# Interleaving score products with maxima products, and a row-paired output projection, in a two-path attention kernel

## The chip, the cores and the metric

The kernel runs on one core of one Trainium2 chip. The metric is the device time of one execution in microseconds (us), the median of several runs. TensorE (PE in the profile, its weight loads PEld) multiplies, VectorE (DVE) takes maxima and does arithmetic, ScalarE (ACT) does exponentials and copies, GpSimd (POOL) masks and adds, SyncE (SP) issues DMAs. Each engine works through its own instructions in their order and waits on semaphores.

## What is computed

Two attention blocks share one input x (2048 x 512, 32 heads of 16 dimensions). Path A is causal attention within four chunks of 512 tokens, plus a memory carried from chunk to chunk. Path B is full attention over all 2048 tokens. Each has its own weights and its own output projection, and a gate mixes them:

```python
logits = einsum("bhqd,bhkd->bhqk", qs, ks) * scale + mask     # A, per chunk of 512
o = g * a_mem + (1.0 - g) * softmax(logits) @ vs              # A, then  a = o @ wo
scores = einsum("bhqd,bhkd->bhqk", q, k) * (Dh ** -0.5)       # B, all 2048 tokens
b = (softmax(scores) @ v).transpose(...).reshape(B, S, D) @ wo
out = g * a + (1 - g) * b
```

## The kernel before, in words

**Units.** The work is cut into 32 units of path A and 32 of path B; a unit is four heads and 512 queries. After a first part (projections of q, k and v, about 330 us) the main loop runs k = 0 to 31; turn k does unit k of A and unit 32 + k of B.

**Groups.** A turn has 37 groups, n = 0 to 36, recorded by `t_group`. Groups 0 to 31 are of B: two groups for each of 16 tiles of 128 keys, two heads in each. Groups 32 to 36 are of A. A group of B is one *T product* for each of its two heads (L528): 64 rows of contraction (16 dimensions as a rounded part and a rest, and rows that subtract the maximum), 128 keys by 512 queries, into one PSUM bank each. Head j = 0 uses rows 0 to 63 of the array (here the *low half*), head j = 1 rows 64 to 127 (the *high half*), so that the two run side by side. ScalarE then takes the exponential of each bank (L534) into SBUF, and the bank is free again. T products use three banks in turn (tb0, tb1, mb), the one used longest ago first.

**Products with V.** `pvs` records them behind each group (L550): for the key tile before, four heads side by side in four strips of 32 columns of the array, summed over all key tiles in the bank pvb. That is another tiling of the array than that of T.

**Maxima.** The maximum that T subtracts is found one turn ahead. A *maxima task* for a unit of B (`s_b`, L474) is a pair of products, queries by 512 keys, high half first, into one of two PSUM tiles of two banks (sbk0 and sbk1, taken in turn); VectorE reduces both banks in one instruction (L476), and the tile is free again. `s_a` (L452, with mask products L456, reduced at L460 and L462) does it for A. A table `plan` gives the tasks to groups: B's 32 tasks one each to groups 20 to 31 of one turn and groups 0 to 19 of the next, A's six to groups 32 to 36. `m_chain` (L485 to L495, VectorE) joins them behind group 21, and `m_rows` transposes them on TensorE behind group 24 (L501). A group is recorded in this order: its T products, its maxima tasks, what `extras` adds, its products with V.

**Output projection.** `out_mm` (L616) does one of 24 parts, one per turn from k = 9, in group 1 (for k = 31 two): 12 products over all 128 rows of contraction into a bank of T. Odd turns do A's weights and copy the sum to SBUF (L620, ScalarE); even turns do B's, add that copy (L623, VectorE) and store the rows.

**Ends of units.** `fin_copy` (L557, VectorE) saves a unit of A in group 0 of the next turn; `fin_rec` (L574 to L578, VectorE) follows behind groups 11 and 13.

Of the kernel before, what the change touches and what calls it, by code (L numbers as in the profile page):

```python
# [7 lines left out]
FT = mybir.dt.float32  # L8
# [4 lines left out]
OP = mybir.AluOpType  # L13
# [21 lines left out]
def gated_mix_kernel(ctx, tc, xt, wq, wk, wv, wo, beta, wqkv, wob, gate_w, out):  # L35
# [477 lines left out]

    GA = (((0, (0, 1)),), ((0, (2, 3)),), ((1, (0, 1)), (3, (0, 1))), ((1, (2, 3)), (3, (2, 3))), ((2, (0, 1)), (2, (2, 3))))

    def t_group(u, n, banks):


        kd, qd, c = UN[u]
        bs = [bank(banks) for _ in range(2)]  # L520
        c0 = 0
        for it, hs in (((n // 2, (n % 2 * 2, n % 2 * 2 + 1)),) if kd == "B" else GA[n]):
            q0 = 128 * it if kd == "A" else 0
            w = C - q0
            pn = it if kd == "B" else it % 2
            for j, h in enumerate(hs):
                r = slice(64 * j, 64 * j + 64)
                nc.tensor.matmul(bs[j][:, c0:c0 + w], k_of(u, h // 2)[r, 128 * it:128 * it + 128],  # L528
                                 q_of(u)[r, h // 2, q0:], start=True, stop=True)
                PT[u, it, h] = PTILE[pn % 2][:, 2 + j if (kd, it) == ("A", 2) else h][:, c0:c0 + w]  # L530
            c0 += w
        for j in range(2):
            pt = PTILE[pn % 2][:, 2 + j if (kd, n) == ("A", 4) else hs[j]]
            nc.scalar.activation(pt, bs[j], AF.Exp, scale=SCALE)  # L534
            if kd == "A":
                m = pt[:, :128] if n < 2 else pt.rearrange("p (a t) -> p a t", a=4)[:, ::3 if n < 4 else 2]
                nc.gpsimd.affine_select(out=m, in_=m, pattern=[[1, 128]] if n < 2 else [[0, 2], [1, 128]],  # L537
                                        compare_op=OP.is_ge, fill=0.0, base=0, channel_multiplier=-1)
# [73 lines left out]
    def out_mm(c, t, a):  # L612

        b = misc()
        for n, (oi, wi, g) in enumerate([(oi, wi, g) for oi, wi in TERMS for g in range(4)]):
            nc.tensor.matmul(b, (AT["oh"], AT["ol"])[oi][:, g, a], (AT["wh"], AT["wl"])[wi][:, g, a],  # L616
                             start=n == 0, stop=n == 11)
        if a == 0:
            AT["yo"] = AT["L"].tile([128, DM], FT, name="yo")
            nc.scalar.activation(AT["yo"], b, AF.Copy)  # L620
        else:
            tt = 4 * c + t
            nc.vector.tensor_tensor(AT["yo"], b, AT["yo"], op=OP.add)  # L623
            nc.sync.dma_start(outr[tt * 128:(tt + 1) * 128, :], AT["yo"])

    def tail_ops(t):
        s = KB[2 * (t // 2)][:, t % 2]
# [247 lines left out]
    def extras(k):  # L875

        pre, post = {}, {}
        if not k:
            for n in range(4):
                pre[2 * n] = [fill[n - 4]]  # L880
        post[2 * S_LAST + 4] = [todo(m_rows, k + 1)]
        for n, at in [(k - 9, 1)] + [(23, 2 * OMI)] * (k == 31):
            if n >= 0:
                pre[at] = [todo(out_mm, n // 8, n // 2 % 4, n % 2)]
        return pre, post

    def beside(k, it):
# [35 lines left out]
    for k in range(31):  # L923
        if k:
            spread([todo(s_b, 33 + k, *t) for t in (sorted(ST_B, key=lambda t: t[2]) if k == 1 else ST_B)],
                   [(k - 1, n) for n in range(2 * S_FIRST, 2 * NT)] + [(k, n) for n in range(2 * S_LAST)])
        else:
            spread(st33[EARLY:], sorted([(0, n) for n in range(2 * S_LAST)] + [(0, 2 * n) for n in range(4)]))
        for n, t in enumerate(ST_A):
            plan.setdefault((k, 2 * NT + n - (n > 2)), []).append(todo(s_a, k + 1, *t))  # L930

    for k in range(32):
        ua, ub = k, 32 + k
        banks = T3 + [b[:, 0] for b in SBK] * (k == 31)
        for n in range(NG):
            it = n // 2 if n < NG - 1 else NT + 2
            t_group(*(ub, n) if n < 2 * NT else (ua, n - 2 * NT), banks)
            for f in plan.get((k, n), []) + ex[k][0].get(n, []):
                f()
            pvs(k, n)  # L940
            for f in ex[k][1].get(n, []):
                f()
            if n % 2 == 0 and n < NG - 1:
                continue
            beside(k, it)
            if it == S_LAST:
                m_chain(k + 1)
            if it == 4 and not k:
                late()
            if it == 4 and not k:  # L950
                load_q(ub + 2)
                for c in range(NC4):
                    load_kb(2, c)
            if it == NT and k < 29:
                load_q(ub + 3)
                load_kb(k + 3)
            if it == 6 and k < 31:
                load_q(ua + 1)
                load_ka(ua + 1)
                if (ua + 1) % 2 == 0:  # L960
                    load_va(ua + 1)
            if it == 9:
                if k % 2 == 0 and k < 30:
                    load_vb(k // 2 + 1)
                if 1 <= k <= 4:
                    load_wo(k - 1)
# [55 lines left out]
```

## Time and profile before

| | us |
|---|---|
| median of 3 runs | 1959.55 (1957.34 to 1963.12) |
| the profiled execution | 1956.4, of which the span of its instructions is 1954.7 |
| busy in it: PE, DVE, ACT, POOL | 1930.3, 1629.9, 1433.4, 275.8 |
| granted TensorE clock | 0.999 |

In the views, a row of the timeline has the start, the time from the first start to the last end, the engine, the line, what is written from what, and the count of instructions that it joins; in brackets stands how long the engine was idle before it and for what. A TensorE product starts in the record about when its weight load starts, and its recorded length holds the time through the array, so the distance from start to start is what it costs. In the page's groups the two numbers behind the bar are the busy time and the mean length in ns of one instruction. A group of B shows as T x2 (or two rows of one), the pair of the maxima task L474 x2, and L550 x8 (four products in two passes each).

### The profile page before, as it was taken

The page shows a single profiled execution, that of the slowest core. Times are in us where ns is not written, and L with a number is a line of the kernel's source. Part 1 is how long each engine was busy: PE and PEld are TensorE (multiplying, and loading weights), DVE is VectorE, ACT ScalarE, POOL GpSimd, SP SyncE. Part 2 cuts the span into 40 slices and gives each one's busy share as a digit, 9 for nine tenths or more (in the row PEclk, how much of TensorE's full clock was granted, in tenths as well). Part 3 has the DMA queues.
Part 4 walks back from the last instruction along what each step waited for, and adds up shares of the span by engine and source line. Part 5 has one row for each costly group of instructions (what it writes and reads, how often), then busy time and mean ns, then how long its engine had stood idle before and what let it go on. Part 6 is the DMA issues. An engine that isn't in the chain of part 4 may idle for free.

```text
span 1954.7 us, 43539 instructions
## 1 busy us (share of the span) xinstructions
PE 1930.3 (99%) x17485; PEld 939.3 (48%) x17485; DVE 1629.9 (83%) x1798; ACT 1433.4 (73%) x2699; POOL 275.8 (14%) x497
## 2 busy tenths in 40 slices
PE   7999999999999999999999999999999999999999
PEld 5887777444344444444444444444444444444445
DVE  7135766899999999999999999999999999999942
ACT  4233333688888888888888888888888888888884
POOL 5201000012120101111111111111111111111022
PEclk9999999999999999999999999999999999999999
DMA  7666655644444444343435453444354444434111
GB/s 218 170 205 188 198 192 178 156 98 115 98 115 93 106 91 109 81 111 80 114 87 115 87 115 87 113 87 115 87 115 87 109 86 96 101 88 106 48 50 58
DMA packets 163790, 222.49 MB, mean 114 GB/s; under 512 B 39916, under 2 KB 90556, under 8 KB 157828
## 3 DMA queue, kind: packets, MB, share of 16 engines
q1 hardware_dynamic: 159284, 211.41, 43.7%
q0 software_dynamic: 3248, 8.03, 2.1%
q8 instruction: 138, 2.26, 0.5%
q14 instruction: 64, 0.52, 0.1%
q10 hardware_dynamic: 1056, 0.26, 0.1%
HBM read 147.95 MB, written 68.16 MB: 111 GB/s over the span
## 4 chain that ended last, share of the span: by engine, by line
PE 95%; DVE 3%; ACT 1%; SPq 1%; DMA 1%; issue 0%; DVEq 0%; ACTq 0%
PE pvb L550 33%; PE tb L528 17%; PE sbk L474 12%; PE mb L528 9%; PE tb L304 4%; PE sbk L452 3%; PE tb L616 2%; PE mb L304 2%; PE sbk L287 1%; DVE mxb L476 1%; PE tb L287 1%; PE pvb L304 1%; PE mb L616 1%; PE sbk L456 1%; PE mb L287 1%; PE pvb L287 1%
## 5 line engine op out<-in xcount | busy, mean ns | idle before, releaser
L476 DVE TENSOR_REDUCE mxb<-sbk 128x2 f32<-128x1024 f32 x1024 | 1222.3, 1222 | 67.3 <-PE sbk L474 63.1
L534 ACT ACTIVATE raw<-tb 128x512 f32<-128x512 f32 x1555 | 887.5, 598 | 152.9 <-PE tb L528 89.6
L550 PE MATMUL pvb<-raw,vb 128*17 128x256 f32 (+1 forms) x8072 | 639.3, 388 | 0.0
L534 ACT ACTIVATE raw<-mb 128x512 f32<-128x512 f32 x782 | 467.6, 598 | 79.5 <-PE tb L528 44.8
L528 PE MATMUL tb<-qb,xh 64*128 64x512 f32 x872 | 331.6, 495 | 1.7 <-ACT raw L534 1.7
L550 PEld LDWEIGHTS pvb<-raw,vb 128*17 128x17 f32 x8072 | 134.4, 95 | 340.1 <-issue 336.6
L474 PE MATMUL sbk<-xh,qb 64*128 64x512 f32 x1344 | 281.5, 395 | 2.7 <-DVE mxb L476 1.8
L528 PE MATMUL mb<-qb,xh 64*128 64x512 f32 x445 | 220.6, 496 | 0.0
L537 POOL TENSOR_SCALAR_AFFINE_SELECT raw<-raw 128x256 f32<-128x256 f32 (+1 forms) x320 | 115.5, 361 | 709.6 <-ACT raw L534 701.7
L528 PEld LDWEIGHTS tb<-qb,xh 64*128 64x128 f32 x872 | 124.7, 183 | 179.6 <-issue 89.9
L528 PE MATMUL tb<-qb,kb 64*128 64x512 f32 x470 | 179.5, 496 | 1.3 <-DVE st L314 0.8
L460 DVE TENSOR_REDUCE mx<-sbk 128x2 f32<-128x768 f32 (+1 forms) x128 | 136.7, 1090 | 22.9 <-PE sbk L456 18.3
L474 PE MATMUL sbk<-kb,qb 64*128 64x512 f32 x704 | 146.4, 398 | 0.0
L474 PEld LDWEIGHTS sbk<-xh,qb 64*128 64x128 f32 x1344 | 138.3, 186 | 7.4 <-DVE mxb L476 5.0
L528 PEld LDWEIGHTS mb<-qb,xh 64*128 64x128 f32 x445 | 81.3, 183 | 95.2 <-issue 50.4
L590 POOL TENSOR_TENSOR o<-o,d 128x512 f32<-128x512 f32 x31 | 39.7, 1281 | 545.6 <-DMA d<-rd 461.9
L528 PEld LDWEIGHTS tb<-qb,kb 64*128 64x128 f32 x470 | 68.2, 183 | 100.1 <-issue 52.6
L528 PE MATMUL mb<-qb,kb 64*128 64x512 f32 x234 | 116.1, 496 | 0.0
L550 PE MATMUL pvb<-raw,va 128*17 128x256 f32 (+2 forms) x1280 | 94.7, 384 | 0.8 <-ACT pvs L559 0.8
L452 PE MATMUL sbk<-ka,qa 64*128 64x256 f32 (+3 forms) x512 | 88.2, 358 | 1.1
L528 PE MATMUL tb<-qa,ka 64*128 64x512 f32 (+3 forms) x339 | 79.5, 372 | 0.0
L311 ACT ACTIVATE st<-tb 128x512 fp32r<-128x512 f32 x33 | 19.8, 599 | 80.2 <-DVE phi L310 40.5
(284 smaller groups left out, 1837.6 us busy)
## 6 DMA issues: line engine op xcount, KB each, us to landing
xh<-dB SPq DMA_DIRECT2D x38, 512.0 KB
vb<-vdB SPq DMA_DIRECT2D x16, 1088.0 KB
dB<-st SPq DMA_DIRECT2D x64, 256.0 KB
dA<-st SPq DMA_DIRECT2D x64, 256.0 KB
pd<-pvs SPq DMA_DIRECT2D x64, 256.0 KB
kb<-dB SPq DMA_DIRECT2D x22, 512.0 KB
xh<-dB SPq DMA_DIRECT2D x38, 256.0 KB
qb<-dB SPq DMA_DIRECT2D x64, 128.0 KB
```

The lines of the kernel that those rows point to most:

```text
L287: nc.tensor.matmul(b, lhs, WV[wi][:, k, :], start=n == 0, stop=n == 11)
L304: nc.tensor.matmul(b, WS[ws][w][wi][:, k, :], (XH, XL)[xi][c][:, k, :], start=n == 0, stop=n == 11)
L452: nc.tensor.matmul(b[:, j, c0:c0 + n], q_of(u)[r, p, i * 128:(i + 1) * 128], k_of(u, p)[r, :n], start=True, stop=False)
L460: nc.vector.tensor_reduce(m[:, :, p, i], b[:, :, :n], axis=AX.X, op=OP.max)
L474: nc.tensor.matmul(b[:, j], q_of(u)[r, p, i * 128:(i + 1) * 128], k_of(u, p)[r, kc * C:(kc + 1) * C], start=True, stop=True)
L476: nc.vector.tensor_reduce(MXB[u][:, :, p, i, kc], b, axis=AX.X, op=OP.max)
L528: nc.tensor.matmul(bs[j][:, c0:c0 + w], k_of(u, h // 2)[r, 128 * it:128 * it + 128], q_of(u)[r, h // 2, q0:], start=True, stop=True)
L534: nc.scalar.activation(pt, bs[j], AF.Exp, scale=SCALE)
L537: nc.gpsimd.affine_select(out=m, in_=m, pattern=[[1, 128]] if n < 2 else [[0, 2], [1, 128]], compare_op=OP.is_ge, fill=0.0, base=0, channe ...
L550: nc.tensor.matmul(PVB[32 * h:32 * h + E + 1, q0 + lo:q0 + hi], vt[:, it, 4 * q + h, :], pt[:, lo:hi], start=it == 0 and lo == 0, stop=it ...
L590: nc.gpsimd.tensor_tensor(o, o, d, op=OP.mult)
L616: nc.tensor.matmul(b, (AT["oh"], AT["ol"])[oi][:, g, a], (AT["wh"], AT["wl"])[wi][:, g, a], start=n == 0, stop=n == 11)
```

## The change

Two parts. First, `t_group` takes the group's maxima tasks as `between` and records them after its first T product, ahead of its second. The task's pair is high half, low half, so a group of B now reads: T low, task high, task low, T high. Groups without a task, those of A, and group 1 from k = 9 are as before. Second, for k = 9 to 30 the projection is done by `out_rows` in place of `out_mm`: 24 products of 64 rows, low and high half by turns, into the two banks of an sbk tile, in the order of the maxima tasks' tiles. The two halves of the sum are then joined outside TensorE: ScalarE copies one bank, VectorE copies or adds the other, and in even turns GpSimd adds twice ahead of the store. The maxima task of group 2 of these turns is moved to the last group (36) of the turn before, and in group 1 the projection is recorded ahead of the maxima task, no longer behind it.

```diff
-    def t_group(u, n, banks):
+    def t_group(u, n, banks, between=()):
             for j, h in enumerate(hs):
+                if j:
+                    for f in between:
+                        f()
                 r = slice(64 * j, 64 * j + 64)
                 nc.tensor.matmul(bs[j][:, c0:c0 + w], k_of(u, h // 2)[r, 128 * it:128 * it + 128],
                                  q_of(u)[r, h // 2, q0:], start=True, stop=True)
+    def out_rows(c, t, a):
+        b = rot("s", SBK)
+        for n, (oi, wi, g) in enumerate([(oi, wi, g) for oi, wi in TERMS for g in range(4)]):
+            for j in range(2):
+                r = slice(64 * j, 64 * j + 64)
+                nc.tensor.matmul(b[:, j], (AT["oh"], AT["ol"])[oi][r, g, a], (AT["wh"], AT["wl"])[wi][r, g, a],
+                                 start=n == 0, stop=n == 11)
+        if a == 0:
+            AT["y"] = [AT["L"].tile([128, DM], FT, name=n) for n in ("yo", "yp")]
+            nc.scalar.activation(AT["y"][0], b[:, 0], AF.Copy)
+            nc.vector.tensor_copy(AT["y"][1], b[:, 1])
+        else:
+            tt = 4 * c + t
+            y0, y1 = AT["y"]
+            y2 = AT["L"].tile([128, DM], FT, name="yq")
+            nc.scalar.activation(y2, b[:, 0], AF.Copy)
+            nc.vector.tensor_tensor(y1, b[:, 1], y1, op=OP.add)
+            nc.gpsimd.tensor_tensor(y0, y0, y2, op=OP.add)
+            nc.gpsimd.tensor_tensor(y0, y0, y1, op=OP.add)
+            nc.sync.dma_start(outr[tt * 128:(tt + 1) * 128, :], y0)
-                pre[at] = [todo(out_mm, n // 8, n // 2 % 4, n % 2)]
+                pre[at] = [todo(out_rows if k < 31 else out_mm, n // 8, n // 2 % 4, n % 2)]
+    for k in range(9, 31):
+        plan[k - 1, NG - 1] += plan.pop((k, 2))
-            t_group(*(ub, n) if n < 2 * NT else (ua, n - 2 * NT), banks)
-            for f in plan.get((k, n), []) + ex[k][0].get(n, []):
+            mid = plan.pop((k, n)) if n < 2 * NT and (k, n) in plan and (k < 9 or n != 1) else []
+            t_group(*(ub, n) if n < 2 * NT else (ua, n - 2 * NT), banks, mid)
+            own, tasks = ex[k][0].get(n, []), plan.get((k, n), [])
+            for f in own + tasks if k else tasks + own:
                 f()
```

What it does to TensorE's order is seen from the end of turn 9 to group 4 of turn 10. In the rows, L528 and L550 of before are L531 and L553 of the changed kernel; sbk is the maxima tile, tb and mb the banks of T, pvb that of the products with V, wh, wl, oh and ol the rounded parts and rests of weights and outputs, and the brackets hold the engines waited for. Before, from the last products with V of group 36 (turn 9) on:

```order
L550 MATMUL pvb<-raw_86,va_76 17x128 x4
L528 MATMUL tb_111<-qb_68,xh_87 128x512 [waits DMAHW1_49,DMAHW0_49]
L528 MATMUL tb_110<-qb_68,xh_87 128x512 [waits Activation_49]
L474 MATMUL sbk_114<-xh_88,qb_69 128x512 [waits DVE_49]
L474 MATMUL sbk_114<-xh_88,qb_69 128x512
L550 MATMUL pvb<-raw_86,va_76 17x256 [waits Pool_49] x2
...
L474 MATMUL sbk_115<-xh_88,qb_69 128x512
L616 MATMUL tb_110<-wh,oh 128x512 [waits Activation_49]
L616 MATMUL tb_110<-wh,oh 128x512 x3
L616 MATMUL tb_110<-wl,oh 128x512 x4
L616 MATMUL tb_110<-wh,ol 128x512 x4
L528 MATMUL mb<-qb_68,xh_87 128x512 [waits Activation_49]
```

The same stretch of the changed kernel, from the mask products of group 36 on:

```order
L456 MATMUL sbk_114<-cmask,crows 128x64
L474 MATMUL sbk_115<-xh_88,qb_69 128x512 [waits DVE_49]
L474 MATMUL sbk_115<-xh_88,qb_69 128x512
L553 MATMUL pvb<-raw_86,va_76 17x384 [waits Pool_49] x4
...
L531 MATMUL mb<-qb_68,xh_87 128x512 [waits Activation_49]
L634 MATMUL sbk_115<-wh,oh 128x512 [waits DVE_49]
L634 MATMUL sbk_115<-wh,oh 128x512 x7
L634 MATMUL sbk_115<-wl,oh 128x512 x8
L634 MATMUL sbk_115<-wh,ol 128x512 x8
L474 MATMUL sbk_114<-xh_88,qb_69 128x512 [waits DVE_49]
L474 MATMUL sbk_114<-xh_88,qb_69 128x512
L531 MATMUL tb_111<-qb_68,xh_87 128x512 [waits Activation_49]
```

A maxima task stands in group 36 now, ahead of its products with V; the projection follows T of group 1 directly, with the task behind it, and takes the tile sbk_115 that the moved task had, so that group 3's task is the next to need it. An ordinary group of B (turn 10, group 4) read, before:

```order
L528 MATMUL tb_111<-qb_68,xh_87 128x512 [waits Activation_49]
L528 MATMUL tb_110<-qb_68,xh_87 128x512 [waits Activation_49]
L474 MATMUL sbk_114<-xh_88,qb_69 128x512 [waits DVE_49]
L474 MATMUL sbk_114<-xh_88,qb_69 128x512
L550 MATMUL pvb<-raw_86,vb_2773 17x256 x3
```

and in the changed kernel:

```order
L531 MATMUL tb_110<-qb_68,xh_87 128x512 [waits Activation_49]
L474 MATMUL sbk_114<-xh_88,qb_69 128x512 [waits DVE_49]
L474 MATMUL sbk_114<-xh_88,qb_69 128x512
L531 MATMUL mb<-qb_68,xh_87 128x512 [waits Activation_49]
L553 MATMUL pvb<-raw_86,vb_2773 17x256 x3
```

The wait for ScalarE that frees the second T bank moved behind the task, and the wait for VectorE that frees the sbk tile moved ahead of the second T product. On VectorE, from the last A maxima of turn 9 on, with the joining of the projection's sums (L623 before, L645 after; pvs is `fin_copy`), before:

```order
L462 TENSOR_REDUCE mx<-sbk_115 128x4 [waits PE_49]
L476 TENSOR_REDUCE mxb<-sbk_114 128x2 [waits PE_49]
L557 COPY pvs<-pvb 128x512 [waits DMAHW1_49,DMAHW5_49,PE_49,Activation_49]
L476 TENSOR_REDUCE mxb<-sbk_115 128x2 [waits PE_49]
L623 TENSOR_TENSOR yo<-tb_110,yo 128x512 [waits PE_49,Pool_49]
```

and in the changed kernel:

```order
L462 TENSOR_REDUCE mx<-sbk_114 128x4 [waits PE_49]
L476 TENSOR_REDUCE mxb<-sbk_115 128x2 [waits PE_49]
L476 TENSOR_REDUCE mxb<-sbk_114 128x2 [waits PE_49]
L560 COPY pvs<-pvb 128x512 [waits DMAHW1_49,DMAHW5_49,PE_49,Activation_49]
L645 TENSOR_TENSOR yp<-sbk_115,yp 128x512 [waits Activation_49]
```

The addition reads the second bank of the sbk tile and waits for ScalarE, which reads the first (the copy L644), where before it waited for TensorE alone of the two; the reduction of group 1's task stands behind it.

## The prediction

> **What bounds the kernel now.** I read the page first, then the busy time of one late turn, then that turn's timelines engine by engine.
>
> ```profile
> span 1954.7 us, 43539 instructions
> PE 1930.3 (99%) x17485; PEld 939.3 (48%) x17485; DVE 1629.9 (83%) x1798; ACT 1433.4 (73%) x2699; POOL 275.8 (14%) x497
> 1032.10:1082.14 50.04, 50.01 (x508) 21.25 (x505) 46.80 (x48) 40.88 (x77) 7.45 (x14) 1.00 0.49 113
> ```
>
> The third row is turn 14: length, busy time of PE, PEld, DVE, ACT and POOL, granted clock. TensorE never rests and its clock is full, but VectorE is busy for 46.8 of 50.0 us, so it is a close second: what TensorE gains can be taken back by VectorE. Where TensorE's time goes is read from starts:
>
> ```profile
> 1038.13 0.50 PE L528 MATMUL mb<-qb,xh 64*128 64x512 f32 x1
> 1038.47 0.40 PE L474 MATMUL sbk<-kb,qb 64*128 64x512 f32 x2
> 1038.80 0.63 PE L550 MATMUL pvb<-raw,vb 128*17 128x256 f32 x8
> ...
> 1054.08 0.50 PE L528 MATMUL tb<-qb,xh 64*128 64x512 f32 x1
> ...
> 1058.99 0.52 PE L528 MATMUL tb<-qb,xh 64*128 64x512 f32 x2
> ...
> 1060.41 0.50 PE L528 MATMUL mb<-qb,xh 64*128 64x512 f32 x1
> ...
> 1064.09 0.49 PE L528 MATMUL mb<-qb,xh 64*128 64x512 f32 x1
> ...
> 1065.54 0.49 PE L528 MATMUL mb<-qb,xh 64*128 64x512 f32 x1
> 1065.76 0.49 PE L528 MATMUL tb<-qb,xh 64*128 64x512 f32 x1
> ...
> 1074.34 0.49 PE L528 MATMUL tb<-qa,ka 64*128 64x512 f32 x1
> ```
>
> Group 3 starts at 1038.13: T to task 0.34, task to products with V 0.33, these to the next T 0.55, together 1.22 (I carry 1.218). Groups 3 to 31 (up to 1074.34, the first of A) take 36.21; 29 x 1.218 is 35.32, so 0.89 is lost. Of it 0.23 lies between groups 24 (1064.09) and 25 (1065.54), where `m_rows` stands, 0.22 in group 25, whose second T (1065.76) waits for its bank, and 0.20 in group 20 (1058.99 to 1060.41), the first with the next unit's data. The other 0.24 are delays of a few hundredths a group, which I put down to the second T bank too.
>
> **Part one, task between the T products.** No instruction is added. The floor of 1.218 should stand: four streams of 64 rows, two side by side, in either order, then the same change of tiling. Does low half beside high half of another kind run as well? Turn 2, whose group 2 has no products with V ahead of it, shows both:
>
> ```profile
> 447.64 0.40 PE L474 MATMUL sbk<-kb,qb 64*128 64x512 f32 x2
> 447.88 0.39 PE L528 MATMUL tb<-qb,xh 64*128 64x512 f32 x1
> 448.55 0.50 PE L528 MATMUL tb<-qb,xh 64*128 64x512 f32 x1 [0.29 <-ACT raw L534]
> 448.56 0.73 PE L474 MATMUL sbk<-kb,qb 64*128 64x512 f32 x2
> ```
>
> A pair follows another after 0.24, and a T that waited starts 0.01 from a task's product. So the second T is needed only 0.34 after the first, and its bank waits vanish: a gain of 0.22 + 0.24 = 0.46 a turn. ScalarE loses nothing: T is done 0.50 after its start, so the second bank is there 0.34 after the first, while the first one's exponential (0.6, as the copy L620 below) still runs. Group 20's 0.20 stays.
>
> The price is VectorE. The task's tile must now be free when the group starts, where the product itself began 0.34 later and its weight load 0.1. How near is that?
>
> ```profile
> 1049.85 0.24 DVE L574 RECIPROCAL rec<-rec 128x16 f32<-128x16 f32 x1
> ...
> 1050.22 2.35 DVE L476 TENSOR_REDUCE mxb<-sbk 128x2 f32<-128x1024 f32 x2
> 1052.49 0.24 DVE L574 RECIPROCAL rec<-rec 128x16 f32<-128x16 f32 x1
> ...
> 1052.91 6.87 DVE L476 TENSOR_REDUCE mxb<-sbk 128x2 f32<-128x1024 f32 x6
> ...
> 1061.19 1.23 DVE L476 TENSOR_REDUCE mxb<-sbk 128x2 f32<-128x1024 f32 x1
> 1062.34 0.21 DVE L485 TENSOR_REDUCE mx<-mxb 128x16 f32<-128x64 f32 x1
> ...
> 1062.99 5.98 DVE L476 TENSOR_REDUCE mxb<-sbk 128x2 f32<-128x1024 f32 x5
> ```
>
> One reduction takes 1.22; queued, they start (6.87 - 1.22) / 5 = 1.13 apart. In an even stretch it starts 0.78 after its group (1061.19 for 1060.41) and ends 2 x 1.22 - 0.78 - 1.22 = 0.44 ahead of the group after the next, which takes its tile. The one from 1052.91 ends at 1054.13 and frees the tile of group 16, which starts at 1054.08: 0.05 late. That from 1062.99 ends at 1064.21, for group 24 at 1064.09: 0.12 late. Both follow small work on VectorE (`fin_rec`, `m_chain`). Until now this cost nothing. From the end of a reduction to the weight load that it frees:
>
> ```profile
> 1075.28 2.53 DVE L460 TENSOR_REDUCE mx<-sbk 128x2 f32<-128x1024 f32 x2 [0.16 <-PE sbk L456]
> ...
> 1077.86 0.18 PEld L452 LDWEIGHTS sbk<-ka,qa 64*128 64x128 f32 x2 [0.15 <-DVE mx L460]
> ```
>
> 1077.81 to 1077.86, 0.05. And without the delays above TensorE arrives some 0.05 earlier at the first place and 0.03 at the second. So 0.15 + 0.20 = 0.35 a turn is lost. Net gain 0.11 a turn; in turns 1 to 30 with it, 3.3 us. Turns 1 to 8 would also gain part of the wait at 448.55, but there VectorE has two reductions and `fin_copy` to get through, and group 3's task, needed at once, waits for them; I count nothing.
>
> **Part two, the projection.** Before:
>
> ```profile
> 1031.11 1.06 PE L550 MATMUL pvb<-raw,va 128*17 128x384 f32 x16
> ...
> 1033.32 0.50 PE L528 MATMUL tb<-qb,xh 64*128 64x512 f32 x2
> 1033.66 0.40 PE L474 MATMUL sbk<-kb,qb 64*128 64x512 f32 x2
> 1033.98 1.19 PE L616 MATMUL mb<-wh,oh 128*128 128x512 f32 x4
> 1035.01 1.07 PE L616 MATMUL mb<-wl,oh 128*128 128x512 f32 x4
> 1035.92 1.07 PE L616 MATMUL mb<-wh,ol 128*128 128x512 f32 x4
> 1036.92 0.50 PE L528 MATMUL tb<-qb,xh 64*128 64x512 f32 x2
> ```
>
> From group 1's T (1033.32) to group 3's (1038.13) are 4.81, to group 4's 4.81 + 1.22 = 6.03. One product of 512 columns costs 0.91 / 4 = 0.23 (1035.01 to 1035.92). After: T to the first pair 0.34, 12 pairs at 0.23 make 2.76 (24 products, two side by side), the task 0.23, group 2's T to its products with V 0.33, these 0.55: group 3 starts after 4.21, 0.60 earlier, because two changes of tiling and the task of group 2 are gone. Two things give it back.
>
> First, the moved task. Group 36's V products (1031.11) would have to wait for it: its tile is that of the fifth A task, whose reduction ends late:
>
> ```profile
> 1029.89 2.04 DVE L462 TENSOR_REDUCE mx<-sbk 128x4 f32<-128x1024 f32 x2 [0.22 <-PE sbk L456]
> 1037.02 0.69 DVE L623 TENSOR_TENSOR yo<-mb,yo 128x512 f32<-128x512 f32 x1 [1.19 <-PE mb L616]
> ```
>
> The first of these two lasts as long as a 1024-element one, 1.22, to 1031.11; plus 0.05 for the weight load, plus 0.34 + 0.10 for load, stream and change of tiling (as T to task, and task to V less a stream of 0.23): V starts at 1031.60, 0.49 late.
>
> Second, the joining. VectorE's addition reads the same sbk tile as ScalarE's copy and waits for the copy, which the order shows. How such a pair runs is seen at the end of the kernel, where both engines read halves of one bank:
>
> ```profile
> 1948.08 0.42 DVE L654 COPY raw<-tb 128x256 f32<-128x256 f32 x1 [0.97 <-PE tb L643]
> 1948.60 0.39 ACT L652 ACTIVATE raw<-tb 128x256 f32<-128x256 f32 x1 [1.01 <-DVE raw L654]
> L620 ACT ACTIVATE yo<-tb 128x512 f32<-128x512 f32 x7 | 4.2, 598 | 15.4 <-PE tb L616 15.4
> L616 PE MATMUL mb<-wl,oh 128*128 128x512 f32 x32 | 8.6, 390 | 0.0
> ```
>
> One after the other, 0.10 apart. Counted from group 1's T: last pair at 0.34 + 11 x 0.23 = 2.87, done 0.39 later, 3.26; copy from 3.30 to 3.90; addition (0.69, row 1037.02) from 3.95 to 4.64; the tile free for group 3's task at 4.69, wanted at 4.21: 0.48 late. Group 4 starts at 4.21 + 1.22 + 0.48 = 5.91. The reduction of group 1's task, behind the addition, ends at 4.56 + 1.22 = 5.78, in time for group 4. So 6.03 - 5.91 = 0.12 is gained, 0.49 lost: 0.37 a turn, 22 turns, 8.1 us lost. VectorE idled for 1.19 ahead of L623, which covers its longer work; GpSimd's two additions and the later store lie in its idle 86%, and delay no load that is wanted before group 13. ScalarE's copy lies in the time in which TensorE does the projection.
>
> **The sum.** 8.1 - 3.3 = 4.8 us longer than the profiled execution's 1956.4: 1961.2. That execution lies 3.15 below the median of the runs shown, so I forecast 1964.3, 0.25% slower. About 0.3% (5.9 us) is what a measurement can tell from no change.
>
> **A rule against the change.** At 447.64 the next pair came after 0.24, less than load and stream together (0.34, from 1033.32 to 1033.66): its weights came in while the same half was streaming. The Trainium skill, "TensorE: Matmul & The Clock Gate", Part 3, says that weight loads overlap with products in flight only when the row group differs. By that rule each pair would cost 0.34 and the sum would be 29 us longer (rival 3); by the row it stays. The trace disagrees with the rule, but with one follow-on pair, not with twelve.
>
> **Rivals.**
> 1. *The waits don't bite.* If the group 3 wait is hidden (ScalarE and VectorE read the two banks at once, so 0.48 falls away, 22 turns, 10.6 us), the kernel takes 1953.7; if VectorE also keeps ahead at groups 16 and 24 (0.35 x 30 = 10.5), 1943.2. For it: the banks differ. Against: the pair 1948.08, 1948.60 and the order. Chance 0.20.
> 2. *VectorE sets the pace*, which ends far on the slow side. Between groups 11 and 24 it must make up 0.37 + 0.42 + 0.65 (the gaps that `fin_rec` and `m_chain` leave between reductions) with 13 x (1.218 - 1.13) = 1.14 and the margin of 0.44 less 0.05: nothing is to spare. If queued reductions came 1.16 apart, 13 x 0.03 = 0.39 more would be lost a turn, 11.7 us: 1976. It decides from about 1.14 on; also if group 3's wait leaves VectorE behind up to group 11. For it: 46.8 of 50.0 us busy. Against: the even 1.13. Chance 0.24.
> 3. *The projection's pairs don't follow each other without a gap*, each paying load and stream, 0.34 for 0.23: 12 x 0.11 x 22 = 29 us, 1993. Against: the 0.24 at 447.64. Chance 0.04.
> 4. *The change does not do what it says*: bank waits move to other places, and the halves' gain and loss cancel; 1957 to 1962. Chance 0.07.
>
> The forecast itself, 1959 to 1970, has 0.45; somewhat over half of it lies within 5.9 us of before. Faster: most of rival 1, 0.17. Slower: 0.19 of the forecast, 0.22 of rival 2, rival 3: 0.45. Same: the rest, 0.38. The range leaves out rival 3, the far end of rival 1 and the worst of rival 2: 1950 to 1978.
>
> **What would show it.** Step by step in the changed profile: second T of a group 0.34 behind the first, never waiting for ScalarE; groups 16 and 24 with a task that waits for VectorE by 0.15 to 0.20; group 25 without its 0.22; 12 projection pairs in 2.76; V of group 36 0.5 later; VectorE's L645 starting when ScalarE's copy ends, and group 3 waiting for it by about 0.5. I am wrong if a group's floor leaves 1.218, if the projection's pairs take more than 0.23, or if group 3 does not wait.

## The result, and the profile after

The changed kernel takes 1956.37 us, median of 21 runs, beside 1958.73 for the kernel before in the same comparison: a ratio of 0.9991, 95% interval 0.9984 to 0.9997. By the ratio it is 1.8 us faster, 0.09%; forecast were 1964.3 and 0.25% slower. The ratio leaves out one run of each kernel that took far longer (4083.00 and 2725.53), and it is not the quotient of the two medians, which lie 2.4 apart. The change is within 0.3%, but a forecast loss of 4.8 us has become a small gain.

The page of the changed kernel, and turn 14 (columns as in the prediction):

```profile
span 1955.4 us, 44154 instructions
PE 1931.4 (99%) x17749; PEld 937.4 (48%) x17749; DVE 1629.5 (83%) x1809; ACT 1442.9 (74%) x2710; POOL 304.9 (16%) x519
```

```profile
1034.83:1084.91 50.08, 50.04 (x522) 21.26 (x518) 46.40 (x49) 41.91 (x78) 10.04 (x15) 1.00 0.48 114
```

Turn 14 is 0.04 longer than before, TensorE as busy as it was and VectorE 0.4 less, so this row alone does not tell where the forecast loss went. The steps are seen in TensorE's timeline of that turn, at the projection and at groups 3, 16, 20, 24 and 25:

```profile
1033.40 0.51 PE L474 MATMUL sbk<-kb,qb 64*128 64x512 f32 x2
1033.84 1.06 PE L553 MATMUL pvb<-raw,va 128*17 128x384 f32 x16
...
1036.38 1.09 PE L634 MATMUL sbk<-wh,oh 64*128 64x512 f32 x8
...
1039.14 0.41 PE L474 MATMUL sbk<-kb,qb 64*128 64x512 f32 x2
...
1040.27 0.49 PE L531 MATMUL mb<-qb,xh 64*128 64x512 f32 x1
1040.73 0.50 PE L474 MATMUL sbk<-kb,qb 64*128 64x512 f32 x2
...
1056.56 0.50 PE L531 MATMUL tb<-qb,xh 64*128 64x512 f32 x1
1056.72 0.57 PE L474 MATMUL sbk<-kb,qb 64*128 64x512 f32 x2
...
1061.60 0.50 PE L531 MATMUL tb<-qb,xh 64*128 64x512 f32 x1
1061.60 0.73 PE L474 MATMUL sbk<-xh,qb 64*128 64x512 f32 x2
1061.94 0.39 PE L531 MATMUL tb<-qb,xh 64*128 64x512 f32 x1
1062.26 0.63 PE L553 MATMUL pvb<-raw,vb 128*17 128x256 f32 x8
1062.82 0.50 PE L531 MATMUL mb<-qb,xh 64*128 64x512 f32 x1
...
1066.47 0.49 PE L531 MATMUL mb<-qb,xh 64*128 64x512 f32 x1
1066.65 0.55 PE L474 MATMUL sbk<-xh,qb 64*128 64x512 f32 x2
...
1068.07 0.49 PE L531 MATMUL mb<-qb,xh 64*128 64x512 f32 x1
...
1069.29 0.50 PE L531 MATMUL tb<-qb,xh 64*128 64x512 f32 x1
```

Four places lose, as forecast: the first T and its task start together in an even group, but lie 0.46, 0.16 and 0.18 apart in groups 3, 16 and 24, where the task waits for VectorE; and the moved task starts late and keeps back the products with V behind it. For groups 16 and 24 VectorE shows it:

```profile
1055.45 9.36 DVE L476 TENSOR_REDUCE mxb<-sbk 128x2 f32<-128x1024 f32 x8
...
1065.38 3.48 DVE L476 TENSOR_REDUCE mxb<-sbk 128x2 f32<-128x1024 f32 x3
```

The first reduction of each row takes 1.22, so it ends at 1056.67 and 1066.60, and the tasks follow 0.05 later, at 1056.72 and 1066.65. Two places gain (rows of TensorE above): group 25 lasts 1.22 (1068.07 to 1069.29), as forecast, and group 20 lasts 1.22 as well (1061.60 to 1062.82). That one was forecast to keep its 1.42.

One turn is a small sample. This table gives each group's mean length in turns 10 to 29 of one profile, from the start of its first T product to that of the next group; "A" is the rest of the turn, from the first A group's T to the next turn. "Order alone" and "rows alone" are experiments 1 and 2.

| us | before | changed | order alone | rows alone |
|---|---|---|---|---|
| group 1, with the projection | 3.69 | 3.30 | 3.61 | 3.31 |
| group 2 | 1.22 | 0.89 | 1.22 | 0.91 |
| group 3 | 1.23 | 1.72 | 1.22 | 1.48 |
| group 16 | 1.24 | 1.36 | 1.36 | 1.24 |
| group 20 | 1.43 | 1.22 | 1.22 | 1.45 |
| group 24 | 1.45 | 1.60 | 1.60 | 1.45 |
| group 25 | 1.44 | 1.22 | 1.22 | 1.44 |
| A | 7.82 | 8.29 | 7.81 | 8.30 |
| the other 25 groups | 30.68 | 30.49 | 30.48 | 30.70 |
| turn | 50.18 | 50.08 | 49.74 | 50.27 |

A turn is 0.10 shorter, where the prediction made it 0.26 longer.

### The profile page after: what moved, and what is told of

Its sections match the earlier page's. It is cut to its first block, busy times and chain, and to the rows that moved or that the text cites. A ratio compares the mean times of both kernels' runs of the same rounds, so it can differ in the third digit from the quotient of the medians.

```text
span 1955.4 us, 44154 instructions
## 1 busy us (share of the span) xinstructions
PE 1931.4 (99%) x17749; PEld 937.4 (48%) x17749; DVE 1629.5 (83%) x1809; ACT 1442.9 (74%) x2710; POOL 304.9 (16%) x519
## 4 chain that ended last, share of the span: by engine, by line
PE 94%; DVE 2%; DMA 2%; SPq 1%; issue 1%; ACT 1%; DVEq 0%; ACTq 0%
PE pvb L553 33%; PE tb L531 17%; PE sbk L474 12%; PE mb L531 9%; PE tb L304 4%; PE sbk L634 3%; PE sbk L452 3%; PE mb L304 2%; PE sbk L287 1%; PE tb L287 1%; PE pvb L304 1%; PE sbk L456 1%; PE mb L287 1%; PE pvb L287 1%; SPq L394 1%
## 5 line engine op out<-in xcount | busy, mean ns | idle before, releaser
L553 PE MATMUL pvb<-raw,vb 128*17 128x256 f32 (+1 forms) x8072 | 639.9, 388 | 0.0
L474 PE MATMUL sbk<-xh,qb 64*128 64x512 f32 x1344 | 463.2, 446 | 3.7 <-DVE mxb L476 2.2
L531 PE MATMUL tb<-qb,xh 64*128 64x512 f32 x865 | 345.1, 441 | 0.0
L553 PEld LDWEIGHTS pvb<-raw,vb 128*17 128x17 f32 x8072 | 135.0, 95 | 344.1 <-issue 338.7
L474 PE MATMUL sbk<-kb,qb 64*128 64x512 f32 x704 | 233.7, 445 | 0.3
L531 PEld LDWEIGHTS tb<-qb,xh 64*128 64x128 f32 x865 | 143.5, 185 | 171.6 <-issue 95.0
L531 PE MATMUL mb<-qb,xh 64*128 64x512 f32 x452 | 204.1, 452 | 0.0
L474 PEld LDWEIGHTS sbk<-xh,qb 64*128 64x128 f32 x1344 | 184.5, 184 | 15.7 <-DVE mxb L476 6.6
L531 PE MATMUL tb<-qb,kb 64*128 64x512 f32 x462 | 184.8, 442 | 1.3 <-DVE st L314 0.9
L531 PEld LDWEIGHTS mb<-qb,xh 64*128 64x128 f32 x452 | 83.3, 184 | 95.6 <-issue 51.2
L531 PEld LDWEIGHTS tb<-qb,kb 64*128 64x128 f32 x462 | 77.0, 184 | 91.8 <-issue 52.5
L531 PE MATMUL mb<-qb,kb 64*128 64x512 f32 x242 | 109.5, 453 | 0.0
L474 PEld LDWEIGHTS sbk<-kb,qb 64*128 64x128 f32 x704 | 93.0, 184 | 9.2 <-issue 3.4
L553 PE MATMUL pvb<-raw,va 128*17 128x256 f32 (+2 forms) x1280 | 94.7, 384 | 0.8 <-ACT pvs L562 0.8
```

Source lines behind the costliest of these rows:

```text
L474: nc.tensor.matmul(b[:, j], q_of(u)[r, p, i * 128:(i + 1) * 128], k_of(u, p)[r, kc * C:(kc + 1) * C], start=True, stop=True)
L553: nc.tensor.matmul(PVB[32 * h:32 * h + E + 1, q0 + lo:q0 + hi], vt[:, it, 4 * q + h, :], pt[:, lo:hi], start=it == 0 and lo == 0, stop=it ...
```

## The experiments

All ratios are to the kernel before, with 95% intervals. The kernel before was timed again beside each set of experiments (medians 1958.48 to 1959.65), so a difference in us is worked out from the ratio, times 1959. The theory after the comparison: the order gains what was forecast and also group 20's 0.20, because the wait instructions of that group's task are then worked off before the group begins. The rival: the projection was costed too high.

### 1 and 2. Each part alone

Part one alone, against the changed kernel:

```diff
-    for k in range(9, 31):
-        plan[k - 1, NG - 1] += plan.pop((k, 2))
...
-                pre[at] = [todo(out_rows if k < 31 else out_mm, n // 8, n // 2 % 4, n % 2)]
+                pre[at] = [todo(out_mm, n // 8, n // 2 % 4, n % 2)]
...
-            mid = plan.pop((k, n)) if n < 2 * NT and (k, n) in plan and (k < 9 or n != 1) else []
+            mid = plan.pop((k, n)) if n < 2 * NT and (k, n) in plan else []
...
-            for f in own + tasks if k else tasks + own:
+            for f in tasks + own:
```

> Only part one: the tasks between the T products in every turn; the projection and its tasks as before. Ratios are to the kernel before (about 1958.7 us). Theory (the step on group 20 was wrong: its 0.20 goes as well, and turn 0 costs about 3.3): 30 x (0.11 + 0.20) = 9.3 less, 3.3 more, so 6.0 less: 1952.7, ratio 0.997. Rival (part one brings only the 0.11 a turn of the prediction, and the projection was costed too high): 3.3 less, 3.3 more: 1958.7, ratio 1.000.

Measured: 1948.97, ratio 0.9946 (0.9931 to 0.9962), 10.6 us less. That is more than the theory's 6.0, and far from the rival's 0.

Part two alone:

```diff
-            mid = plan.pop((k, n)) if n < 2 * NT and (k, n) in plan and (k < 9 or n != 1) else []
+            mid = []
```

> Only part two: the projection as 64-row pairs with its moved task; every task again behind both T products. Theory (0.37 lost in each of 22 turns): 8.1 more, 1966.8, ratio 1.004; T pairs 12 in 2.76, V of group 36 0.5 late, group 3 0.46 late. Rival (the projection's price was too high, or is hidden where the second T waits): 1958 to 1960, ratio 1.000.

Measured: 1960.67, ratio 1.0006 (0.9998 to 1.0015), 1.2 us more: the rival's size. The two parts don't add up: -10.6 and +1.2 make -9.4, and the changed kernel has -1.8. The table says where. On top of the new order, part two costs 50.08 - 49.74 = 0.34 a turn, close to the 0.37 of the prediction. On the old order it costs 0.09, because group 3 takes 1.48 there instead of 1.72. TensorE in that group, rows alone:

```profile
1040.67 0.49 PE L531 MATMUL mb<-qb,xh 64*128 64x512 f32 x1
1040.90 0.50 PE L531 MATMUL tb<-qb,xh 64*128 64x512 f32 x1
1041.14 0.49 PE L474 MATMUL sbk<-kb,qb 64*128 64x512 f32 x2
1041.56 0.63 PE L553 MATMUL pvb<-raw,vb 128*17 128x256 f32 x8
```

The second T goes ahead while the task waits for its tile; in the new order it stands behind the task and waits with it.

The other surprise of the order alone is group 1. In the kernel before it lasts 3.60 in even turns and 3.78 in odd ones, and the prediction had read turn 14. TensorE and ScalarE at the start of turn 15 before:

```profile
1083.36 0.50 PE L528 MATMUL tb<-qb,kb 64*128 64x512 f32 x1
1083.54 0.50 PE L528 MATMUL mb<-qb,kb 64*128 64x512 f32 x1
```

```profile
1081.94 1.06 ACT L609 ACTIVATE oh<-o 128x1024 fp32r<-128x1024 f32 x1
```

Every other turn starts with `out_split`'s copy on ScalarE, 1.06 long, and group 1's second T waits 0.18 behind the exponentials that it delays. With either part the 0.18 is gone (3.61 and 3.31 in every turn). Behind a task the second T is wanted later: in turn 15 of the order alone the exponential that frees its bank ends at 1081.99, and the T starts at 1082.21. With the moved task ScalarE gets the 0.47 by which the products with V are late: in turn 15 of the rows alone that exponential ends at 1086.49, ahead of group 1 at 1086.58. A mean of 0.09 a turn was thus missing from the gain.

### 3. Turn 0

The changed kernel with turn 0 in the order of before:

```diff
-            mid = plan.pop((k, n)) if n < 2 * NT and (k, n) in plan and (k < 9 or n != 1) else []
+            mid = plan.pop((k, n)) if k and n < 2 * NT and (k, n) in plan and (k < 9 or n != 1) else []
```

> The changed kernel with turn 0 in the order of before (all tasks behind both T products); turns 1 to 31 as changed. Theory (turn 0, where groups 0, 2, 4 and 6 have two tasks and a job of the projections, loses 3.3): turn 1 starts 3.3 earlier than in the changed kernel, 1956.4 - 3.3 = 1953.1, ratio to before 0.997. Rival (the 3.4 by which turn 1 starts later come from the projection stage ahead of it): ratio as the changed kernel's, 0.999.

Measured: 1954.29, ratio 0.9971 (0.9960 to 0.9982), against the changed kernel's 0.9991. The ratio is the theory's, but its account of it does not hold: the 3.3 came from comparing one profile of each kernel. Over all profiles of this study, turn 0 lasts 63.01 to 63.05 in the old order (seven profiles) and 63.84 to 63.89 in the new (five). Only the changed kernel's own profile has 65.43, with one job of the projections 1.5 longer, which did not come again. So the new order costs **0.8** there. In the order alone, groups 2, 4, 6 and 19 of that turn, which have two tasks each, last 0.17 to 0.25 longer, since the second T stands behind both; groups 8 and 24, whose task waits for VectorE, last 0.24 and 0.19 longer; groups 20 and 25 give 0.15 and 0.13 back. What makes up the rest of the 3.9 us between the two ratios, which come from different comparisons, stays open.

What else varies from profile to profile follows no edit: turn 0 starts at 334.75 to 342.64, turn 3 lasts 47.2 to 50.7, and turn 8 47.5 to 48.5. VectorE in the changed kernel's profile, turns 3 and 8:

```profile
525.87 1.28 DVE L495 SCALAR_TENSOR_TENSOR m<-mx,mhi 128x32 f32<-128x32 f32 x1
```

```profile
754.56 0.25 DVE L577 RECIPROCAL rec<-rec 128x16 f32<-128x16 f32 x1 [0.49 <-DMA rec<-pd]
```

In turn 3 one instruction of `m_chain` takes 1.28 (0.18 in turn 14), and group 24 lasts 3.04; in turn 8 `fin_rec` waits 0.49 for its load, and group 16 lasts 1.84. Between kernels, means of turns 10 to 29 are compared, which hold few such places, and small ones.

### 4. Group 20 in the old order

```diff
-            mid = plan.pop((k, n)) if n < 2 * NT and (k, n) in plan and (k < 9 or n != 1) else []
+            mid = plan.pop((k, n)) if (n != 20 or not k) and n < 2 * NT and (k, n) in plan and (k < 9 or n != 1) else []
```

> The changed kernel with one group of each turn from 1 on, group 20, in the old order: both T products, then the task. Theory (the task's four instructions that wait for loads, 0.106 apart, stand behind a second T that waits for its bank, and so cost 0.20; ahead of that T they are hidden): group 20 takes 1.42 again instead of 1.22, 30 x 0.20 = 6.0 more than the changed kernel: 1962.4, ratio to before 1.002. Rival (the 0.20 went because TensorE reaches the group at another time, or the loads land earlier): group 20 stays at 1.22, ratio 0.999.

Measured: 1963.85, ratio 1.0020 (1.0010 to 1.0030), 5.7 us above the changed kernel's ratio, for a theory of 6.0; a turn takes 50.29 instead of 50.08. Group 20 takes 1.44 again. TensorE there, turn 14:

```profile
1068.42 0.52 PE L531 MATMUL tb<-qb,xh 64*128 64x512 f32 x2
1068.79 0.57 PE L474 MATMUL sbk<-xh,qb 64*128 64x512 f32 x2
1069.29 0.63 PE L553 MATMUL pvb<-raw,vb 128*17 128x256 f32 x8
1069.84 0.49 PE L531 MATMUL mb<-qb,xh 64*128 64x512 f32 x1
```

From the task to the products with V are 0.50, where 0.33 is usual. The trace also records TensorE's semaphore instructions, which the views leave out. The four of group 20's task wait for seven of the eight queues that load the next unit's Q and K (the second weight load itself waits for the eighth). Their starts, in the trace of the changed kernel and of this one:

```
changed kernel, group starts 1061.59:   1060.821  1060.932  1061.238  1061.344   (51 ns each)
group 20 old, group starts 1068.42:     1068.443  1068.554  1068.680  1068.785   (51 ns each)
```

What they stand behind is seen on ScalarE, which frees the banks, in the changed kernel and in this one:

```profile
1060.18 0.59 ACT L537 ACTIVATE raw<-tb 128x512 f32<-128x512 f32 x1
```

```profile
1067.80 0.60 ACT L537 ACTIVATE raw<-tb 128x512 f32<-128x512 f32 x1 [0.19 <-PE tb L531]
```

With the task ahead of the second T, the wait instructions stand behind the first T alone. Its bank is free at 1060.77, and they are through before the group begins, while products with V still run. In the old order they stand behind the second T as well, whose bank is free at 1068.40. They start only with the group, 0.11 to 0.13 apart, and the task's second weight load comes 0.23 after its first (1068.630 and 1068.861), where a group without such waits has them 0.003 apart.

### 5. The same waits in another group

The kernel of 4, in which group 19's task first reads a little of the next unit's Q and K (the result is overwritten by the task):

```diff
+        for j in (1, 0):
+            if n19:
+                r = slice(64 * j, 64 * j + 64)
+                nc.tensor.matmul(b[:, j, :64], q_of(u + 1)[r, 0, :128], k_of(u + 1, 0)[r, :64], start=True, stop=True)
...
+    for k in range(1, 30):
+        plan[k, 19] = [todo(s_b, 33 + k, *ST_B[-1], True)]
```

> The kernel that had group 20 in the old order (ratio 1.002, group 20 at 1.44), with two small products of 64 columns added ahead of group 19's task that read the next unit's Q and K; their result is overwritten by the task. The eight queues that group 20's task waited for are then waited for in group 19, between its T products; nothing else changes. Theory (group 20's 0.20 is the time of those wait instructions, which stood behind a second T that waits for its bank): group 20 returns to 1.24 although its task stands behind both T products, group 19 grows only by the small products, about 0.07; ratio 1.000. Rival (group 20's 0.20 belongs to the order of its own products or to its bank): it stays at 1.44, ratio 1.002 or above.

Measured: 1960.41, ratio 1.0004 (0.9991 to 1.0016). Group 20 takes 1.22 with both T products ahead of its task. Group 19 takes 1.33, 0.11 more for the small products; its wait instructions start at 1059.68 to 1060.22, before the group begins at 1060.38. TensorE in group 20 (L535 is T, L478 the task, L557 the products with V):

```profile
1061.71 0.51 PE L535 MATMUL tb<-qb,xh 64*128 64x512 f32 x2
1062.06 0.39 PE L478 MATMUL sbk<-xh,qb 64*128 64x512 f32 x2
1062.38 0.63 PE L557 MATMUL pvb<-raw,vb 128*17 128x256 f32 x8
1062.93 0.50 PE L535 MATMUL mb<-qb,xh 64*128 64x512 f32 x1
```

So the 0.20 is the waits' and not that of the products' order or of their bank.

### 6. Group 20 alone

The kernel before, with the new order in group 20 only (the edit of `t_group` is the change's):

```diff
-            t_group(*(ub, n) if n < 2 * NT else (ua, n - 2 * NT), banks)
-            for f in plan.get((k, n), [])
+            mid = plan.pop((k, n), []) if k and n == 20 else []
+            t_group(*(ub, n) if n < 2 * NT else (ua, n - 2 * NT), banks, mid)
+            for f in plan.get((k, n), [])
```

> The kernel before with one edit: in turns 1 to 31 the task of group 20, and of no other group, stands between its T products. Theory: group 20 takes 1.22 instead of 1.425, 30 x 0.2 = 6 less: ratio 0.997. Rival (the new order of all groups around it is needed): group 20 stays above 1.40, ratio 1.000.

Measured: 1951.82, ratio 0.9963 (0.9949 to 0.9977), 7.2 us less, for a theory of 6; group 20 takes 1.22, every other group is as before, and a turn takes 49.98 instead of 50.18. This one edit is worth more than the whole change.

### 7. Groups 16 and 24

The kernel of 3 with these groups in the old order:

```diff
-            mid = plan.pop((k, n)) if n < 2 * NT and (k, n) in plan and (k < 9 or n != 1) else []
+            mid = plan.pop((k, n)) if k and n not in (16, 24) and n < 2 * NT and (k, n) in plan and (k < 9 or n != 1) else []
```

> Turn 0 as before, and in turns 1 to 31 groups 16 and 24 in the old order (both T products, then the task); all other groups as changed. In the changed kernel group 16 takes 1.36 and group 24 1.60, where before they took 1.24 and 1.45. Theory (the task stands 0.34 nearer to the group's start than VectorE's reduction allows there, and nowhere else): both return to 1.24 and 1.45, and group 25 stays at 1.22, so 0.12 + 0.15 = 0.27 less a turn, 8 us less than the kernel that had only turn 0 as before (ratio 0.997): ratio 0.993. Rival (VectorE stays behind, and the next group with its task ahead waits in their place): groups 17, 18 or 25, 26 become longer by as much, ratio 0.997.

Measured: 1949.61, ratio 0.9952 (0.9935 to 0.9969). Group 16 returns to 1.24 and group 24 to 1.45, group 25 stays at 1.22; of group 16's 0.12, 0.03 comes back in group 17 (1.25). A turn takes 49.86, 0.22 less than the changed kernel's; forecast was 0.27. The timed difference to 3 is 3.7 us; the turns' 0.22 would make 6.6, within the two intervals.

### 8. The joining by one engine

ScalarE copies both banks in one instruction:

```diff
-            y0, y1 = AT["y"]
-            y2 = AT["L"].tile([128, DM], FT, name="yq")
-            nc.scalar.activation(y2, b[:, 0], AF.Copy)
-            nc.vector.tensor_tensor(y1, b[:, 1], y1, op=OP.add)
+            y0 = AT["y"][0]
+            y2 = AT["L"].tile([128, 2, DM], FT, name="yq")
+            nc.scalar.activation(y2, b, AF.Copy)
             nc.gpsimd.tensor_tensor(y0, y0, y2, op=OP.add)
-            nc.gpsimd.tensor_tensor(y0, y0, y1, op=OP.add)
...
+            nc.gpsimd.tensor_tensor(y0[:, 0], y0[:, 0], y0[:, 1], op=OP.add)
...
```

(and for the first half, one copy of both banks in place of the two.)

> The changed kernel, where ScalarE alone copies both banks of the projection's tile in one instruction of 1024 columns (1.06 us, as its other copy of that size takes), and GpSimd does all additions; VectorE no longer reads it. In the changed kernel ScalarE's copy and VectorE's addition run one after the other and free the tile 0.46 after group 3 wants it. Theory (the joining is what group 3 waits for): the tile is free 1.06 + 0.05 after the copy's start instead of 1.38, so group 3 takes 1.22 + 0.19 = 1.41 instead of 1.72, 22 x 0.3 = 6.6 less than the changed kernel: ratio to before 0.996. Rival (group 3 waits for VectorE's queue or for ScalarE's exponentials, which now stand 0.46 longer behind the copy): ratio 0.999 or above.

Measured: 1955.90, ratio 0.9984 (0.9975 to 0.9993). Group 3 takes 1.64, not 1.41. In the changed kernel, ScalarE and VectorE:

```profile
1039.35 0.60 ACT L644 ACTIVATE yq<-sbk 128x512 f32<-128x512 f32 x1 [1.63 <-PE sbk L634]
```

```profile
1039.98 0.69 DVE L645 TENSOR_TENSOR yp<-sbk,yp 128x512 f32<-128x512 f32 x1 [2.58 <-ACT yq L644]
```

One after the other, to 1040.67; group 3's task starts at 1040.73. With one reader, ScalarE and TensorE:

```profile
1038.61 1.02 ACT L643 ACTIVATE yq<-sbk 128x1024 f32<-128x1024 f32 x1 [1.59 <-PE sbk L634]
1039.53 1.08 ACT L537 ACTIVATE raw<-tb 128x512 f32<-128x512 f32 x2
```

```profile
1039.52 0.50 PE L531 MATMUL mb<-qb,xh 64*128 64x512 f32 x1
1039.68 0.56 PE L474 MATMUL sbk<-kb,qb 64*128 64x512 f32 x2
1040.17 0.50 PE L531 MATMUL tb<-qb,xh 64*128 64x512 f32 x1
1040.60 0.63 PE L553 MATMUL pvb<-raw,vb 128*17 128x256 f32 x8
```

The task's wait falls to 0.16, as the theory had it. But the second T now waits for its bank: ScalarE's exponential, which stands behind the longer copy, frees it at 1040.12 (in the trace, the first of the two from 1039.53), and that T comes 0.49 after the task instead of 0.34. The products with V then come 0.43 after it, instead of 0.32; why is open. The joining is the cause of group 3's wait, and the remedy runs into the rival for most of its gain.

### 9. The moved task behind the products with V

```diff
-        plan[k - 1, NG - 1] += plan.pop((k, 2))
+        ex[k - 1][1].setdefault(NG - 1, []).extend(plan.pop((k, 2)))
```

> The changed kernel with the moved task behind the products with V of group 36 instead of ahead of them. In the changed kernel the stretch from the first A group to the next turn takes 8.29 instead of 7.82, since those products stand behind a task whose tile VectorE frees late. Theory (a task that stands behind the products with V costs only its 0.23): the stretch returns to 7.82 + 0.23 or less, 22 x 0.25 to 0.47 = 5 to 10 less than the changed kernel: ratio to before 0.994 to 0.996. Rival (its reduction now starts some 0.8 later, VectorE idles as long, and group 0's task or the projection's tile is late instead): what the stretch gains, groups 0 and 1 lose: ratio 0.999.

Measured: 1955.80, ratio 0.9981 (0.9971 to 0.9990). A takes 8.14 and group 0 1.11, 0.26 less together, but group 1 takes 3.46 instead of 3.30. VectorE:

```profile
1032.00 2.03 DVE L462 TENSOR_REDUCE mx<-sbk 128x4 f32<-128x1024 f32 x2 [0.23 <-PE sbk L456]
1034.75 2.36 DVE L476 TENSOR_REDUCE mxb<-sbk 128x2 f32<-128x1024 f32 x2 [0.72 <-PE sbk L474]
```

It idles 0.72 for the moved task, and the projection's tile, which that reduction frees, comes late: the rival for more than half of it.

### 10. All findings, with and without the projection's pairs

First 3, 7, 8 and 9 together (their edits as above):

> All that the findings point to at once: task between the T products from turn 1 on, but not in groups 16 and 24; ScalarE alone copies the projection's tile; the moved task behind the products with V. If the three gains add up (0.27 in 30 turns, 0.3 and 0.25 to 0.47 in 22 turns, on ratio 0.997 for turn 0 as before): 8 + 6.6 + 5 to 10 less, ratio 0.984 to 0.987, about 1930. Rival (VectorE is next: of 50 us it is busy for 46.8, and a shorter turn makes its reductions late at more groups): less than half of that is seen, ratio 0.991 or above.

Measured: 1945.93, ratio 0.9933 (0.9920 to 0.9945), a turn 49.69. The rival's region, though not for its reason: 0.22 (experiment 7), 0.05 and 0.09 (8 and 9) a turn, on 50.08, would make 49.72, so the parts add up, but 8 and 9 bring little. Then part one without turn 0 and without groups 16 and 24, on the old projection:

```diff
-            mid = plan.pop((k, n)) if n < 2 * NT and (k, n) in plan and (k < 9 or n != 1) else []
+            mid = plan.pop((k, n)) if k and n not in (16, 24) and n < 2 * NT and (k, n) in plan else []
```

(with the other lines of 1)

> Part one alone, in turns 1 to 31 and not in groups 16 and 24; the projection and its tasks as before. Theory (on top of the new order part two loses 0.34 a turn, 49.74 with part one alone against 50.08 with both, and the two groups cost 0.27): turns 10 to 29 take 49.74 - 0.27 = 49.47 instead of 50.18 before; 22 x 0.72 + 8 x 0.48 = 19.7 less than before: ratio 0.990, about 1939, faster than every other kernel here. Rival (the shorter turn runs into VectorE, so that other groups wait): 49.7 a turn, ratio 0.994.

Measured: 1939.02, ratio 0.9900 (0.9880 to 0.9919). Turn 14 of it:

```profile
1031.53:1080.99 49.46, 49.42 (x508) 20.79 (x504) 46.55 (x48) 40.83 (x77) 7.45 (x13) 1.00 0.50 114
```

Turns 10 to 29 take 49.49 on average; 49.47 was forecast. It is the fastest kernel of the study, 17 us below the changed one, although VectorE is now busy for 46.55 of 49.46.

## Why the prediction was wrong, step by step

The step that failed is one sentence on part one: "Group 20's 0.20 stays." Group 20's length was read rightly and its cause was not looked for: the semaphore instructions, in TensorE's own order behind a waiting second T. Putting the task ahead of that T removes 0.21 in each of 29 turns, 6.0 us, and the miss is 4.8 + 1.8 = 6.6. Experiment 4 takes the gain back, 6 brings it alone, and 5 moves the waits. That one term comes so near to the whole miss is partly luck: other rows of the table miss by up to 2.5, some each way.

Step by step, in us for the whole kernel (less is faster):

| step | predicted | measured, from the profiles |
|---|---|---|
| second T's waits: group 25 (29 turns) and small delays (30 turns) | -13.8 | -11.8 (0.22 and 0.18 a turn) |
| group 16 (30 turns) and group 24 (29 turns) | +10.5 | +8.0 (0.12 and 0.15) |
| group 20, 29 turns | 0 | -6.0 (0.21) |
| groups 1 to 3 with the projection, 22 turns | -2.6 | -5.1 (0.23) |
| V of group 36, 22 turns | +10.8 | +10.4 (0.47) |
| turn 0 | 0 | +0.8 |
| groups 2 and 3 in turns 1 to 8 | 0 | +0.8 (0.10) |
| sum | +4.9 | -2.9 |

Groups 20 to 31 of turn 30 have no task, since no turn follows that needs their maxima, so groups 20, 24 and 25 change in turns 1 to 29; the prediction took 30 for every row of part one. The measured rows are means of turns 10 to 29 taken for all turns, and miss the timed -1.8 by 1.1. In the two profiles turns 1 to 30 are 2.7 shorter than before; with turn 0's 0.8 it is -1.9. The rest lies in places that one profile has and the next has not: about 1 in turns 3 and 8, as experiment 3 shows, and 0.5 in group 16 of turns 1 and 2 (1.62 and 1.64), where `fin_rec` waits 0.16 and 0.18 for its load; turns 15 and 30 give some 0.5 back.

**Floor and order.** Right: groups keep 1.22, the second T follows the task, and group 25's wait is gone. The two late tasks are late by 0.16 and 0.18 (forecast 0.15 and 0.20), for the reason given: each follows 0.05 behind the reduction that frees its tile, and in the old order these reductions cost next to nothing (experiment 7). The small delays of the second T were forecast at 0.24 a turn, and 0.18 of them went.

**The projection.** Right in its parts: 12 pairs from 1036.38 to 1039.14 are 2.76, V of group 36 waits behind its task, and group 3 waits 0.46 (forecast 0.48) for a joining done one engine after the other. The rule that the prediction quotes from the Trainium skill, "TensorE: Matmul & The Clock Gate", Part 3, would have each pair pay for its weight load, since the row group of a half does not change from pair to pair. The trace disagrees with that rule over the full length: 0.23 a pair, no more than the streams. (The same part of the Trainium skill also lets a load go ahead of products in flight into a background weight buffer; no run here shows which of the two a load is, and the prediction did not weigh it.) Groups 1 to 3 now take 5.91, as forecast. The term was mis-sized in what is taken away: they took 6.14 before, not 6.03, so that 0.11 a turn more was gained than forecast. Of it 0.09 is group 1, which was measured in turn 14 and is 0.18 longer in odd turns.

**Rivals.** VectorE did not become the bound: between groups 11 and 24 only 16 and 24 are late, as forecast, and the fastest kernel has VectorE busy for 46.55 of 49.46. Rival 1 failed too: both of its waits are there, and the time came between it and the forecast for a reason that no rival had. Rival 4's time, 1957 to 1962, lies nearest, but the bank waits did not move, they went (group 25 at 1.22).

**Turn 0 and turns 1 to 8.** The prediction does not speak of turn 0, which costs 0.8 (experiment 3). Groups 2 and 3 of turns 1 to 8 were counted at nothing, and cost 0.8 together: group 2 takes 1.70 instead of 1.89, but group 3 takes 1.51 instead of 1.22, the late task that the prediction named there.

## What to carry to other kernels

Where an in-order engine stands at a wait, look at what is queued behind it, wait instructions included: the four wait instructions here cost nothing while the engine is ahead of its work, and 0.20 us when it is not. Explain every excess over a stage's floor before saying that a change leaves it alone, and read a periodic kernel over its whole period, not in one turn. An order that lets independent work pass a late task also hides what makes the task late, so a loss found for one order is not the loss in another: two edits that share a wait don't add up.

## What the runs showed of the hardware

- Wait instructions on TensorE take 51 ns each and start 0.11 to 0.13 apart when they are worked off one behind the other; four of them cost 0.20 of the group at whose start they stand (1.44 for 1.22, experiment 4), and nothing when products are still running.
- Two small products of 64 columns, one in each row half, lengthened their group by 0.11 (experiment 5).
- One ScalarE copy of 1024 columns over two banks took 1.02. One of 512 takes 0.60, and two exponentials of 512 in a row take 1.08 (row 1039.53 of experiment 8). By these rows one instruction saves an estimated 0.06 against two in a row.
- With identical instructions ahead of it, turn 0 started between 334.75 and 342.64 from one profiled execution to another: single profiles of two kernels cannot be compared in that stretch to better than some us.
